# A gated linear-attention and feed-forward kernel: early weight sums of M2, their stores' queue, and the order of the residual loads

## The chip, the cores and the metric

The kernel runs on one core of one Trainium2 chip. The metric is the device time of one execution in microseconds (us). Before the change the median of three runs is 762.07 us (761.8 to 762.79).

The core has five engines that run their own instruction streams in order: TensorE (PE: matmuls into PSUM), VectorE (DVE), ScalarE (ACT), GpSimd (POOL) and SyncE (SP, which here only starts DMA transfers). ScalarE and GpSimd can start transfers too; each such start is an instruction in their streams. Engines wait for each other, and for transfers, by semaphores. Transfers started by SP and ScalarE share eight semaphores in turn: a transfer that takes one over first waits until the transfer that used it before has landed.

## What is computed

```python
x = A_x; xn = layernorm(x)                       # [1, 2048, 1024]
q, k, v = split(xn @ wqkv)                       # 32 heads of 32
s = (phi(q) @ (phi(k)^T v)) / (phi(q) @ sum phi(k)) @ wo     # linear attention
g = silu((silu(xn @ w_gate) * (xn @ w_up)) @ w_down)         # F = 3584
return x + s * g
```

## The kernel before, in words

Up to about 246 us the kernel does the layer norm and the attention; it writes s to a DRAM buffer, s_dram. After that comes the feed-forward part, in two **passes** over 1024 tokens each (p = 1, then p = 0). Every product there is done with seven block products instead of eight (a Winograd form of Strassen's method), so each weight tile needs four sums of its blocks, T1 to T4.

**Weights in packs.** Gate and up weights, and w_down, are read raw once; their sums are made during the first pass, and what results goes to DRAM as packs (pk_g, pk_u for gate and up, and wd: "a" packs with four quarters and "b" packs with three). All packs travel through one pool, wgu, of eight buffers (tile name w_sb). load_w_to(n) (L270) issues loads up to the n-th pack of a fixed list; each waits until the buffer it gets has been released by its last readers. In the first pass SP's order is the scheduler's, within the due points at which the program calls load_w_to; in the last pass's gate and up part SP's order is the one written down. The other engines follow the written order throughout.

**Each pass** first does 28 gate and up steps (i = 0 to 27, two per 256 columns of F). Then the first pass multiplies by w_down in emit_down (L1220), with token tiles in two pairs (hf = 0: tiles 0, 1; hf = 1: tiles 2, 3). Each pair runs over k = 0 to 13, the second tile LEAD = 6 steps behind the first, so a loop has NS = 20 steps st. There are four loops: "a" products for hf = 0, "a" for hf = 1, then "b" products for hf = 1, which add to the same PSUM banks, and "b" for hf = 0 ("fresh", in new banks). In the a loop of hf = 1 the b packs are loaded, each into the buffer of an a pack that the second tile has just finished (L1365). In the fresh loop the next pass's packs are loaded likewise (L1394).

evac_a (L1272) takes a tile's "a" products out of PSUM: ScalarE copies x (L1282), VectorE adds y and zw (L1283 to L1288), ScalarE applies SiLU (L1290). evac_b (L1294) adds the "b" products (L1302, L1308: tile dd). For hf = 1 the b products write again to the banks dx and dzw that evac_a reads. next_S and emit_Ssum (L705) make sums of activations on VectorE, for the later steps of the loop and for the next pass.

**The last pass** instead uses emit_down_m (L1409): seven products M1 to M7 (order 1, 2, 7, 6, 5, 4, 3), and M1, M2, M4 and M5 are split once more by the same method (l2_M). For these four, sums of w_down's packs are needed again. Those of M1 and M5 are made on GpSimd during the last pass. Those of M2 and M4 are made **early**, in the b loops of the first pass's emit_down, by l2_early (L1118): from b pack j (j = 0 to 6) it makes four sums on VectorE (L1136, 128 x 256) into an unused part of the same buffer, and later stores quarters and sums to DRAM (l2_2, l2_4) with three transfers (L1128 to L1130, 448 KB in all) on SP's queue. The sums of M4 overwrite those of M2. The loop that drives it is L1382 to L1386: M2's sums at steps 3 to 9 of the first b loop, stored three steps later; M4's at steps 10 to 16, stored two steps later.

**Residual tiles.** The end of both passes is fin (L1210): y = y * s (L1214) and x + y (L1215) on VectorE, then the store to the output (L1216), on GpSimd's queue in the first pass and on SP's in the last. x and s come in tiles of 128 x 512 (io_load, L1197: two loads of 128 KB on SP, L1205 and L1206) in a pool of five buffers (iop). There are 32 such tiles in a list fq. Five are loaded during the first pass; after that every fin loads the next one, which must wait until that fin's output has landed, since it takes the same buffer. In emit_down, two fins follow each pair of evac_a, six the hf = 1 b loop, three the fresh loop, and the last three are put off ("deferred") to steps 0, 1 and 2 of the next pass. In emit_down_m, four fins run during M7, four at the start of M3's products (fill3), and eight after that.

Of the kernel before, what the change touches and what calls it, by code (L numbers as in the profile page):

```python
# [21 lines left out]
def kernel(  # L22
# [247 lines left out]
    def load_w_to(n):  # L270
        while w_next[0] < min(n, len(w_seq)):
            load_w()
# [680 lines left out]
    with ExitStack() as p3:  # L953
# [164 lines left out]
        def l2_early(M, j, store):  # L1118

            t = w_tiles[(passes[0], "b", j)][:].rearrange("p h a b -> p (h a b)")  # L1120
            q = M_PACK[M][1]
            w = t[:, 0:6 * CW].rearrange("p (k q c n) -> p q k c n", k=2, q=3, c=2)[:, q]
            T = t[:, 6 * CW:8 * CW].rearrange("p (b n) -> p b n", b=4)
            if store:
                if M not in l2_drams:
                    l2_drams[M] = dram.tile([P, 7, NQ, CH], BF16, name="l2_%d" % M)
                d = l2_drams[M]
                nc.sync.dma_start(out=d[:, 0:2, j], in_=w[:, :, 0])  # L1128
                nc.sync.dma_start(out=d[:, 6, j], in_=w[:, 1, 1])
                nc.sync.dma_start(out=d[:, 2:6, j], in_=T)  # L1130
                return
            r = w.bitcast(F16) if M >= 4 else w
            t1, t2, t3, t4 = [T[:, i].bitcast(F16) for i in range(4)]
            for o_, a_, b_ in ((t1, r[:, 0, 1], r[:, 0, 0]), (t2, r[:, 1, 1], t1), (t3, r[:, 1, 1], r[:, 0, 1]),
                               (t4, r[:, 1, 0], t2)):
                nc.vector.tensor_tensor(out=o_, in0=a_, in1=b_, op=ALU.subtract)  # L1136
# [57 lines left out]
                for t in (2 * hf, 2 * hf + 1):  # L1194
                    fq += [(p, t + TPB, 0), (p, t, 1), (p, t, 0)]

        def io_load(after=None):  # L1197
            if not fq:
                return
            p, t, cc = key = fq.pop(0)  # L1200
            r0 = p * TB2 + t * P
            pool, tg = iop, "io"
            io = pool.tile([P, 2, CW], BF16, name="io", tag=tg)
            eng = nc.sync
            gate([eng.dma_start(out=io[:, 0, :], in_=x2[r0:r0 + P, cc * CW:(cc + 1) * CW]),  # L1205
                  eng.dma_start(out=io[:, 1, :], in_=s_dram[r0:r0 + P, cc * CW:(cc + 1) * CW])],  # L1206
                 after, sync=True)
            io_tiles[key] = io

# [10 lines left out]
        def emit_down(p, h, base, last, more_S, next_S):  # L1220
# [121 lines left out]
                    fin(p, t, 0, g11, *fin_e, cols=cs)  # L1342

            NS = NFG + LEAD
            for hf in range(2):
                t0, t1 = 2 * hf, 2 * hf + 1
                for st in range(NS):
                    if st == 4:
                        while pend:
                            pend.pop(0)()  # L1350
                    if hf == 0:
                        for m in {4: (4,), 8: (5, 6)}.get(st, ()):
                            more_S(m)
                        if st in (12, 14, 16):
                            next_S((st - 12) // 2)
                    elif st % 2 == 0 and 3 <= st // 2 + 2 < NWA:
                        next_S(st // 2 + 2)
                    if st < NFG:
                        step_a(t0, st)
                        if st == NFG - 1:  # L1360
                            evac_a(t0, hf == 0)
                    if st >= LEAD:
                        step_a(t1, st - LEAD)
                        if hf == 1 and (st - LEAD) % 2 == 1:
                            load_w_to(base + NWA + (st - LEAD) // 2 + 2)  # L1365
                evac_a(t1, hf == 0)
                if hf == 0:
                    load_w_to(base + NWA + 1)
# [4 lines left out]
            for hf in (1, 0):  # L1373
                t0, t1 = 2 * hf, 2 * hf + 1
                fresh = hf == 0
                endz = last and fresh
                for st in range(NFG if endz else NS):
                    if st == 4:
                        while pend:
                            pend.pop(0)()  # L1380
                    if not last:
                        for M, q0, dq, lag in zip(L2_EARLY, (3, 10), (1, 1), (3, 2)):  # L1382
                            for d, store in ((0, False), (lag, True)):
                                j, rem = divmod(st + (1 - hf) * NS - q0 - d, dq)
                                if rem == 0 and 0 <= j < NQ:
                                    l2_early(M, j, store)  # L1386
                    if st < NFG:
                        step_b(t0, st, fresh)
                        if st == NFG - 1:
                            fins = evac_b(t0, fresh)  # L1390
                    if st >= LEAD and not endz:
                        step_b(t1, st - LEAD, fresh)
                        if fresh and (st - LEAD) % 2 == 1:
                            load_w_to(base + 2 * NWA + (st - LEAD) // 2 + 2)  # L1394
                if endz:
                    for f in fins:
                        f()
                    finish(t1)
                    break
                fins2 = evac_b(t1, fresh)  # L1400
                for f in fins:
                    f()
                if fresh:
                    deferred.extend(fins2)
                else:
                    for f in fins2:
                        f()

        def emit_down_m(p, h, base):  # L1409
# [165 lines left out]
            for t in range(TPB):  # L1575
                if t:
                    prod_t(7, t, M7[t], True)
                tt(KB[t], M7[t], KA[t])
                flush(1)
            load(7)  # L1580
            sums(S4, A12, S2, ALU.subtract)
            l2_lhs_all(5, quads(h, 0, 1).bitcast(F16), nc.vector)
# [25 lines left out]
            def fill3():  # L1608
                for t in range(TPB):
                    fins.append((t + TPB, 1, silu(T5[t], "g22")))  # L1610
                flush()
                M3.extend(banks())
                out3(0)
# [21 lines left out]
        for pi, p in enumerate(passes):  # L1635
# [81 lines left out]
            for i in range(n):  # L1717
                if first:
                    load_w_to(base + i + (na0 if i < n - 7 else 8 if i > n - 6 else 7))
                else:  # L1720
                    load_w_to(base + i + (5 if i < 17 else 6))
                if i + 1 < n:
                    emit_a(keys[i + 1])
                    emit_c22(keys[i + 1])
# [40 lines left out]
                        l2_lhs(2, quads(h, 1, 0), i // 4 - 1, nc.gpsimd)  # L1765
                if deferred:
                    deferred.pop(0)()
            sp_man.close()
            base += n
            if last_pass:  # L1770
# [37 lines left out]
```

## Time and profile before

| what | value |
|---|---|
| median of 3 runs | 762.07 us |
| the profiled execution: its time, its span | 762.54 us, 760.8 us |
| TensorE busy | 741.0 us, 97% of the span |
| VectorE, ScalarE, GpSimd busy | 592.1, 385.2, 356.4 us |
| DMA, mean over the span | 253 GB/s |
| granted TensorE clock, mean | 0.995 |
| first pass's emit_down | 414.3 to 500.9 us |
| last pass's gate and up steps | 500.9 to 671.8 us |
| emit_down_m, last matmul, end of span | 671.8, 751.05, 760.8 us |

The profile is one execution, recorded by the hardware. "L1242" is line 1242 of the kernel. A row of the timeline gives start, duration, engine, line, operation, output and inputs, how many instructions it merges, and in brackets how long the engine was idle before it and what ended that. "SPq" rows are transfers being started; a transfer lands later. A line of the chain of waits gives start, duration and what ran. A line of the waits of an engine gives the waiting engine and line, who it waited for, total us, times and longest. A line of the table by stretches gives the stretch, its length, then busy us (and instructions) of PE, PEld, DVE, ACT and POOL, the granted clock, the busy share of the 16 DMA engines and GB/s.

### The profile page before, as it was taken

The numbers are of one execution on the slowest core, as the hardware profiler recorded it, in microseconds if no ns is written. First come the engines' busy times: TensorE is split into PE (matmuls) and PEld (weight loads), VectorE is DVE, ScalarE is ACT, GpSimd is POOL, SyncE is SP. The second block draws the span as 40 slices with busy tenths as digits, with TensorE's granted clock in tenths as the row PEclk, the third lists the DMA queues.
The fourth block names the chain that finished last, engine by engine and source line by source line (L and its number), as shares of the span: only waits on it lengthen the run. The fifth ranks groups of instructions, "written<-read, shape, count | busy, mean of one in ns | idle before, by whom it ended". The sixth has DMA issues, their size and how long they took to land.

```text
span 760.8 us, 11165 instructions
## 1 busy us (share of the span) xinstructions
PE 741.0 (97%) x3835; PEld 365.0 (48%) x3899; DVE 592.1 (78%) x1119; ACT 385.2 (51%) x557; POOL 356.4 (47%) x444
## 2 busy tenths in 40 slices
PE   8999999999999999999999999999999999999994
PEld 3544544444544444444444444444444444476582
DVE  6687787886796788888889757767687777778975
ACT  5677776988956565666659201132323222231033
POOL 2444799998540276858675000110764655330000
PEclk9999999999999999999999999999999999999997
DMA  9957799869679667888899249988898875458755
GB/s 315 300 149 135 236 327 306 293 159 276 209 173 307 225 226 270 313 286 313 268 346 400 68 142 315 282 290 314 322 337 280 290 241 173 157 184 290 246 191 159
DMA packets 134425, 192.37 MB, mean 253 GB/s; under 512 B 36480, under 2 KB 108928, under 8 KB 124640
## 3 DMA queue, kind: packets, MB, share of 16 engines
q1 hardware_dynamic: 127024, 160.59, 66.0%
q0 software_dynamic: 5904, 28.58, 9.8%
q10 hardware_dynamic: 1440, 2.49, 1.0%
q8 instruction: 30, 0.49, 0.3%
q14 instruction: 27, 0.22, 0.1%
HBM read 120.85 MB, written 63.44 MB: 242 GB/s over the span
## 4 chain that ended last, share of the span: by engine, by line
PE 88%; DVE 5%; DMA 4%; issue 1%; ACT 1%; SPq 0%; DVEq 0%; ACTq 0%
PE zw L967 25%; PE kv_ps L555 14%; PE xb L967 12%; PE q_ps L183 6%; PE yb L967 6%; PE dzw L1242 5%; PE dm L1481 4%; PE dm L1445 3%; PE fx L817 3%; PE s_ps L775 2%; PE dx L1242 2%; PE dy L1242 2%; DVE w_sb L1136 1%; PE kvz L577 1%; PE nd L744 1%
## 5 line engine op out<-in xcount | busy, mean ns | idle before, releaser
L967 PEld LDWEIGHTS <-w_sb 128*128 128x128 f16 (+1 forms) x1568 | 152.0, 98 | 184.6 <-DMA w_sb<-pk_g 2.0
L967 PE MATMUL xb<-xnT,w_sb 128*128 128x512 bf16 x420 | 113.3, 379 | 1.5
L555 PE MATMUL kv_ps<-wkv_sb,xnT 128*128 128x512 bf16 x499 | 112.9, 379 | 1.2 <-ACT xnT L544 0.4
L967 PE MATMUL zw<-S,w_sb 128*128 128x512 f16 x448 | 105.8, 379 | 0.0
L967 PE MATMUL zw<-xnT,w_sb 128*128 128x512 bf16 x448 | 105.8, 379 | 0.0
L322 POOL TENSOR_TENSOR w_sb<-w_sb 128x512 f16<-128x512 bf16 x42 | 50.7, 1208 | 95.5 <-DVE w_sb L310 51.3
L287 ACT ACTIVATE w_sb<-w_sb 128x2048 bf16<-128x2048 bf16 x42 | 79.9, 1902 | 4.1 <-DMA w_sb<-in_B_w_up_dram 3.0
L555 PEld LDWEIGHTS <-xnT 128*128 128x128 bf16 x512 | 48.3, 98 | 55.9 <-ACT xnT L544 0.8
L967 PE MATMUL yb<-S,w_sb 128*128 128x512 f16 x224 | 57.5, 379 | 1.6 <-DMA w_sb<-pk_g 1.5
L183 PE MATMUL q_ps<-xnT,wq_sb 128*128 128x512 bf16 x249 | 58.0, 379 | 0.8 <-DVE pqT L151 0.4
L1043 ACT ACTIVATE sg<-cg 128x1024 bf16<-128x1024 f32 x28 | 29.6, 1057 | 57.4 <-DVE cg L1036 57.4
L1216 POOL DMA_DIRECT2D out_dram<-io x16 | 8.7, 544 | 106.2 <-DVE io L1215 105.7
L1036 DVE SCALAR_TENSOR_TENSOR cg<-zw,rc_all,s 128x1024 f32<-128x1024 f32 x28 | 35.9, 1283 | 25.4 <-PE zw L967 13.2
L995 DVE SCALAR_TENSOR_TENSOR s<-yb,rc_all,s 128x512 f32<-128x512 f32 x42 | 31.4, 748 | 28.1 <-ACT s L994 28.1
L1148 POOL TENSOR_TENSOR w_sb<-w_sb 128x512 f16<-128x512 bf16 (+3 forms) x32 | 35.9, 1143 | 35.2 <-DMA w_sb<-wd 34.3
L323 POOL TENSOR_TENSOR w_sb<-w_sb 128x512 f16<-128x512 bf16 x42 | 50.8, 1209 | 3.3
L325 POOL TENSOR_TENSOR w_sb<-w_sb 128x512 f16<-128x512 bf16 x42 | 50.4, 1199 | 0.0
L324 POOL TENSOR_TENSOR w_sb<-w_sb 128x512 f16<-128x512 bf16 x42 | 49.9, 1188 | 0.0
L994 ACT ACTIVATE s<-xb,rcl 128x512 f32<-128x512 f32 x14 | 9.6, 687 | 65.8 <-PE xb L967 65.8
L1242 PE MATMUL dx<-w_sb,hT 128*128 128x512 bf16 x108 | 40.9, 379 | 0.2
L994 ACT ACTIVATE s<-xb,rc_all 128x512 f32<-128x512 f32 x42 | 28.4, 676 | 22.9 <-issue 12.7
L310 DVE TENSOR_SCALAR w_sb<-w_sb,cs_all 128x2048 bf16<-128x2048 bf16 x35 | 36.3, 1037 | 2.8
(228 smaller groups left out, 1324.4 us busy)
## 6 DMA issues: line engine op xcount, KB each, us to landing
w_sb<-pk_g SPq DMA_DIRECT2D x27, 1024.0 KB, 6.6
pk_g<-w_sb SPq DMA_DIRECT2D x14, 1024.0 KB, 5.2
w_sb<-pk_u SPq DMA_DIRECT2D x14, 1024.0 KB, 7.6
pk_u<-w_sb POOLq DMA_DIRECT2D x13, 1024.0 KB, 5.4
w_sb<-l SPq DMA_DIRECT2D x12, 896.0 KB, 4.6
w_sb<-in_B_w_gate_dram SPq DMA_DIRECT2D x14, 512.0 KB, 6.6
w_sb<-in_B_w_down_dram SPq DMA_DIRECT2D x28, 256.0 KB, 4.6
w_sb<-in_B_w_up_dram SPq DMA_DIRECT2D x14, 512.0 KB, 5.4
```

The lines of the kernel that those rows point to most:

```text
L183: nc.tensor.matmul(q_ps[:], lhsT=wq_sb[:, dc, g * P:(g + 1) * P], rhs=xn_ap(dc, btok), start=(dc == 0), stop=(dc == DC - 1))
L287: nc.scalar.activation(out=junk, in_=raw_view(key, t), func=ACT.Square, accum_out=asum[:])
L310: nc.vector.tensor_scalar(out=w, in0=w, scalar1=cs_all[:, c:c + 1], scalar2=None, op0=ALU.mult)
L322: nc.gpsimd.tensor_tensor(out=T1, in0=b12, in1=b11, op=ALU.subtract)
L323: nc.gpsimd.tensor_tensor(out=T2, in0=b22, in1=T1, op=ALU.subtract)
L324: nc.gpsimd.tensor_tensor(out=T3, in0=b22, in1=b12, op=ALU.subtract)
L325: nc.gpsimd.tensor_tensor(out=T4, in0=b21, in1=T2, op=ALU.subtract)
L555: mm = nc.tensor.matmul(kv_ps[:], lhsT=xn_ap(dc, tok), rhs=wkv_sb[:, dc, c * CW:(c + 1) * CW], start=(dc == 0), stop=(dc == DC - 1))
L967: mm = nc.tensor.matmul(out, lhsT=lhs(k), rhs=rhs(k), start=(first and k == 0), stop=(k == HK - 1), skip_group_check=True)
L994: nc.scalar.activation(out=s1[:], in_=x_[:], func=ACT.Copy, scale=rc)
L1036: nc.vector.scalar_tensor_tensor(out=d12, in0=zw[:], scalar=rc, in1=s2[:, None, :].to_broadcast([P, 2, TB]), op0=ALU.mult, op1=ALU.add)
L1242: nc.tensor.matmul(out, lhsT=lhs, rhs=rhs, start=first, stop=lastk, skip_group_check=True)
```

## The change

Three edits, none of them to a matmul.

1. l2_early's stores are issued by ScalarE instead of SP, and M2's sums come sooner. Counting steps n through the a loop of hf = 1 (0 to 19) and the two b loops (20 to 59), M2's sums of pack j move from n = 23 + j to n = 8 + 2j, stored two steps later; M4's from n = 30 + j to n = 25 + j, still stored two steps later.
2. Residual loads are held back. After the first of the six fins of the hf = 1 b loop, the following loads wait in a list until step 11 of the fresh loop; those of the deferred fins are issued three steps i later, after that step's load_w_to. So they stand behind pack loads in SP's queue.
3. The last seven residual tiles no longer rotate through the five io buffers. Three are loaded ahead of M5's last loads in the written order, into the dead buffer S2 and two dead buffers of the activation pool; four in fill3, into buffers of the pack pool.

```diff
@@ l2_early
-                nc.sync.dma_start(out=d[:, 0:2, j], in_=w[:, :, 0])
-                nc.sync.dma_start(out=d[:, 6, j], in_=w[:, 1, 1])
-                nc.sync.dma_start(out=d[:, 2:6, j], in_=T)
+                nc.scalar.dma_start(out=d[:, 0:2, j], in_=w[:, :, 0])
+                nc.scalar.dma_start(out=d[:, 6, j], in_=w[:, 1, 1])
+                nc.scalar.dma_start(out=d[:, 2:6, j], in_=T)
@@ io_load
-        def io_load(after=None):
-            if not fq:
+        io_due = deque()
+        hold = [False]
+
+        def io_load(after=None, pool=None, tg=None):
+            if not fq or len(fq) <= 7 and pool is None:
+                return
+            if hold[0] and after is None:
+                io_due.append(hold[0])
                 return
             p, t, cc = key = fq.pop(0)
             r0 = p * TB2 + t * P
-            pool, tg = iop, "io"
-            io = pool.tile([P, 2, CW], BF16, name="io", tag=tg)
-            eng = nc.sync
...
+            if pool is wgu:
+                io = w_slot()[:].rearrange("p h a b -> p (h a b)")[:, 0:2 * CW].rearrange("p (q n) -> p q n", q=2)
+            else:
+                io = (pool or iop).tile([P, 2, CW], BF16, name="io", tag=tg or "io")
...
@@ emit_down
             NS = NFG + LEAD
+            def early(n):
+
+                for M, at, lag in ((2, lambda j: 8 + 2 * j, 2), (4, lambda j: NS + 5 + j, 2)):
+                    for j in range(NQ):
+                        if n in (at(j), at(j) + lag):
+                            l2_early(M, j, n > at(j))
+
             for hf in range(2):
                 t0, t1 = 2 * hf, 2 * hf + 1
                 for st in range(NS):
+                    if not last and hf == 1:
+                        early(st)
...
                     if not last:
-                        for M, q0, dq, lag in zip(L2_EARLY, (3, 10), (1, 1), (3, 2)):
-                            for d, store in ((0, False), (lag, True)):
-                                j, rem = divmod(st + (1 - hf) * NS - q0 - d, dq)
-                                if rem == 0 and 0 <= j < NQ:
-                                    l2_early(M, j, store)
+                        early(NS * (2 - hf) + st)
...
+                        if fresh and st == LEAD + 5:
+                            hold[0] = False
+                            while io_due:
+                                io_due.popleft()
+                                io_load()
...
                 for f in fins:
                     f()
+                    hold[0] = -1 if not fresh and not last else False
@@ emit_down_m, ahead of load(7)
+            io_load(None, sp, "S2")
+            for _ in range(2):
+                io_load(None, xnp, "xn8")
             load(7)
@@ fill3
                     fins.append((t + TPB, 1, silu(T5[t], "g22")))
+                for _ in range(TPB):
+                    io_load(None, wgu)
                 flush()
@@ the last pass's gate and up steps
                     load_w_to(base + i + (5 if i < 17 else 6))
+                    hold[0] = False
+                    while io_due and io_due[0] <= i:
+                        io_due.popleft()
+                        io_load()
+                    hold[0] = i + 3
```

More of the change, by code (lines that the diff above doesn't have):

```diff
@@ L1201, in io_load @@
             r0 = p * TB2 + t * P
-            pool, tg = iop, "io"
-            io = pool.tile([P, 2, CW], BF16, name="io", tag=tg)
-            eng = nc.sync
-            gate([eng.dma_start(out=io[:, 0, :], in_=x2[r0:r0 + P, cc * CW:(cc + 1) * CW]),
-                  eng.dma_start(out=io[:, 1, :], in_=s_dram[r0:r0 + P, cc * CW:(cc + 1) * CW])],
+            if pool is wgu:
+                io = w_slot()[:].rearrange("p h a b -> p (h a b)")[:, 0:2 * CW].rearrange("p (q n) -> p q n", q=2)
+            else:
+                io = (pool or iop).tile([P, 2, CW], BF16, name="io", tag=tg or "io")
+            gate([nc.sync.dma_start(out=io[:, 0, :], in_=x2[r0:r0 + P, cc * CW:(cc + 1) * CW]),
+                  nc.sync.dma_start(out=io[:, 1, :], in_=s_dram[r0:r0 + P, cc * CW:(cc + 1) * CW])],
                  after, sync=True)
@@ L1767 @@
                     deferred.pop(0)()
+            hold[0] = False
+            while io_due:
+                io_due.popleft()
+                io_load()
             sp_man.close()
```

## The prediction

> **What bounds the kernel now.** I read the page first: its engine totals, then the waits of TensorE, then the stretches in which TensorE is idle, then the rows around them.
>
> ```profile
> span 760.8 us, 11165 instructions
> PE 741.0 (97%) x3835; PEld 365.0 (48%) x3899; DVE 592.1 (78%) x1119; ACT 385.2 (51%) x557; POOL 356.4 (47%) x444
> ```
>
> TensorE is busy 741.0 of 760.8 us. No matmul is changed, so only its 20 idle us can be won. The waits of TensorE name two inside the region of the change, and the table by stretches shows the rest:
>
> ```profile
> PE dzw L1242 <- DVE dd L1308: 1.8, 1, 1.8
> PE yb L967 <- DMA w_sb<-pk_g: 1.5, 1, 1.5
> ```
>
> ```profile
> 459.00:485.00 26.00, 24.11 (x111) 10.94 (x112) 21.43 (x67) 4.44 (x6) 1.08 (x2) 1.00 0.98 311
> 751.00:761.00 10.00, 0.05 (x1) 0.00 (x0) 4.67 (x13) 1.45 (x3) 0.00 (x0) 0.61 0.54 166
> ```
>
> The first line of the table says that while VectorE is late (459 to 485 us), the DMA engines are 98% busy. The second says that after 751 us TensorE does nothing: the last ten us are eviction, residual and stores. Of TensorE's other idle time, 4.7 us lie before 250 us, which the change does not touch. So three places can move: the 1.8 at 481 us, the 1.5 at 510.5 us, the 9.7 at the end.
>
> **The end: the last seven residual tiles.** The timelines of TensorE, VectorE and SP after 741 us:
>
> ```profile
> 741.79 9.26 PE L1445 MATMUL dm<-w_sb,hT 128*128 128x512 bf16 x55
> ```
>
> ```profile
> 745.08 0.69 DVE L1433 TENSOR_TENSOR c<-dm,kA 128x512 f32<-128x512 f32 x1 [1.70 <-PE dm L1445]
> 748.28 0.43 DVE L1214 TENSOR_TENSOR g<-g,io 128x512 bf16<-128x512 bf16 x1 [2.51 <-DMA io<-s_dram]
> ...
> 752.27 0.68 DVE L1433 TENSOR_TENSOR c<-dm,kA 128x512 f32<-128x512 f32 x1
> ...
> 757.62 0.23 DVE L1215 TENSOR_TENSOR io<-g,io 128x128 bf16<-128x128 bf16 x1
> ```
>
> TensorE ends at 751.05. VectorE had its operands at 745.8 but sat 2.51 us for a residual tile, because the five io buffers come free only when earlier outputs have landed; then it waited 0.97, 0.19 and 0.79 us more. The change loads these seven tiles into buffers that are dead by then. In the program's order the last four pairs stand behind M3's weights, whose issues end at 730.5 (SP row 724.08, 6.39 us); the latest buffer is freed by a product of M4 that ends near 734.3. With 2.5 us to landing (median of the io loads after 690 us) all seven are there by 739, and the first is used at 745.8. Then: 745.08 + 0.69 = 745.77; five residual pairs last 3.99 us as before (748.28 to 752.27), to 749.76; the next c 0.69, to 750.45 (its matmuls end at 748.0); its SiLU 0.72, to 751.17; one pair 0.80, to 751.97; the last pair in two parts 1.15 (756.70 to 757.85), to 753.1. Before, VectorE ended at 757.85. What follows, 2.95 us to the span's end, stays. **Gain 4.7 us.** What is late next is VectorE itself, 2 us behind TensorE. The cost of the loads is nothing as long as DMA has room, which is 0.44 busy from 729 to 751; without room the first waits come back, up to the 4.7.
>
> **The packs at 510 us.** In SP's order before, the pack loads for the next pass stand behind the early stores and residual loads:
>
> ```profile
> 504.48 0.33 SPq L1205 DMA_DIRECT2D io<-in_A_x_dram  x1
> 504.87 0.44 SPq L1206 DMA_DIRECT2D io<-s_dram  x1
> 505.40 0.39 SPq L264 DMA_DIRECT2D w_sb<-pk_g  x1
> ```
>
> This pk_g lands 6.6 us later and TensorE gets it at 512.08, 1.54 late. Its slot was free after the second tile's fourth step of the last half, near 492. In the changed program's order the first two packs stand ahead of the sixth residual pair, and the other held pairs behind a third pack. Issued at 494 and landing within 9.0 us (the longest pack of this stretch that did not queue behind other packs) it is there by 503: **gain 1.5 us**. The held pairs then come later. What they may delay is VectorE's sixth residual pair, which blocked VectorE to 496.74 before too, with TensorE unharmed: the next eviction is needed at 502.6. ScalarE's last SiLUs of that half now queue behind 42 DMA issues (below) and may slip from 483 to some 487; their banks are needed at 500.9, so this costs nothing.
>
> **The early sums.** Moved: 24 of M2's 28 sums (a row of 40 takes 9.41, so 0.235 us each) go from behind the next pass's S sums to between next_S and the two evictions evac_a; M4's 28 stay, some steps earlier. Moved to ScalarE's queue: 42 stores. ScalarE's own issues cost 0.33 to 0.37 us in this trace (s_dram, L781), 15 us in all, and it is idle 13.9 us before 456 and 10.3 after 466. The gain: VectorE from the second evac_a to dd has 12 sums less, 2.8 us, more than the 1.8 of the wait. But the moved sums bring a **new wait**: M2's sum for pack j waits for b pack j, and VectorE works in order. The loads keep their times, since each waits for an a slot: the sixth is issued at
>
> ```profile
> 459.38 6.67 DMA w_sb<-wd
> ```
>
> ```profile
> 462.81 0.69 DVE L1283 TENSOR_TENSOR s<-dy,s 128x512 f32<-128x512 f32 x1 [3.83 <-PE dzw L1242]
> ...
> 481.66 1.22 DVE L1308 TENSOR_TENSOR dd<-dzw,s 128x1024 f32<-128x1024 f32 x1
> ```
>
> and landed at 466.05, whereas the second evac_a started at 462.81. In the changed order that evac_a stands behind the sixth pack's sums. On ScalarE its copy stands behind the stores of packs 3 to 5, and one of them waits for the semaphore that this very load uses. Behind both stands TensorE: it writes the second tile's dzw again at 467.38.
> Working: landing. These 768 KB loads take 5.7 us in the median (4.8 to 8.2 among the four of this stretch). I take 5.7, so 465.1: the load before it lands sooner, since its SP queue no longer carries stores; but ScalarE's stores now run beside it. Two more issues on ScalarE, 0.8, copy at 465.9; copy to third sum 2.83 (456.15 to 458.98 in the first evac_a): evac_a ends at 468.8 instead of 465.0. TensorE stops for 1.4 us at 467.4. From there to the matmul behind dd: before, 465.02 to 481.66 is 16.64; less 12 sums, 2.82; plus dd to TensorE, 1.28 (482.94 less 481.66): 15.1. So that matmul comes at 483.9 against 482.94: **loss 1.0 us**, and the wait on dd is not gone but has a second one ahead of it. Bounds: with 4.8 to landing the loss is 0.1; with 8.2 it is 3.5; if ScalarE is held by a store that takes 8.9 (the longest of L1128) from 460.4, evac_a ends at 472.5 and the loss is 4.7. If nothing holds evac_a, the gain is the whole 1.8.
> The other moved waits are covered: the first sums delay next_S by 0.9 of 4.5 us that it is early; the first evac_a waits for pack 2 (landed 455.7) and has three us to spare.
>
> The trace shows what one queue does: three stores issued on SP at 463.2 to 464.6 landed after 8 to 9 us, together with the pack issued ahead of them. [...] I know of no row here with stores on ScalarE's queue beside such loads.
>
> **Sum.** The profiled execution took 762.54 (span 760.8 and 1.74 around it), 0.47 above the median of 762.07. -4.7 - 1.5 + 1.0 = -5.2: 757.3 for that execution, **756.9** against the median.
>
> **Rivals.**
> No new wait: the sixth b pack lands by 463.6, evac_a is in time, and the dd wait goes: -4.7 - 1.5 - 1.8 = -8.0, 754.1. For it: DMA is only 0.43 busy from 414 to 459. Against it: none of the four loads took under 4.8.
> Most of it given back: stores or loads at their longest, 3.5 to 4.7 lost: 759.3 to 760.6. For it: 98% busy DMA.
> Slower: the same place, evac_a, with the b pack starved by ScalarE's stores as packs are when queued deep: 14.4 us to landing (the pk_g issued at 508.18). It lands at 473.8, evac_a ends at 477.5, the loss is 477.5 + 15.1 - 482.94 = 9.7: 765.6. It decides once the landing takes more than about 11 us. Against it: only two or three such loads are ever in flight.
> The change does not do what it says: SP stands still on a slot or a semaphore, and the seven tiles come no sooner. Then only +1.0 - 1.5: 761.6.
>
> **How the numbers follow.** About 0.2% (1.5 us) is what a measurement of this kernel can tell from no change. Forecast (loss 0.1 to 3: 756 to 759) 0.48; no new wait 0.2; most given back 0.14; slower 0.09; the tail unchanged 0.09. Range 753.8 to 760.6: it reaches over the first three and leaves out the last two. Faster by over 0.2% (below 760.5): the first three, 0.82; within: 0.10, with a little of the neighbours; slower 0.08.
>
> **What would show it.** Right: after 741 us no VectorE wait on io, and VectorE ends some 2 us after TensorE; no TensorE wait on pk_g; pk_g issued before 496; a TensorE wait on evac_a (L1289 or L1295) of some 1.4 us near 467 and one on dd near 482. Wrong: a b pack that lands before 464 or after 468, a TensorE wait in the first steps of the next pass, or residual pairs that still wait after 745.

## The result, and the profile after

| | before | after |
|---|---|---|
| median of 15 runs | 762.39 us (761.19 to 763.5) | 760.59 us (759.3 to 762.98) |
| the profiled execution: its time, its span | 762.54, 760.8 | 762.85, 761.1 |
| last matmul, VectorE's last instruction | 751.05, 757.85 | 756.06, 758.15 |

The ratio is 0.998 with a 95% interval of 0.997 to 0.9989: a gain of 0.8 to 2.3 us, where 5.2 were forecast. The profiled execution of the changed kernel is one of the longest of its 15, 2.3 above their median. So its trace shows where time was lost, and shows more of it than the median run lost.

First the page and the waits of TensorE:

```profile
span 761.1 us, 11166 instructions
PE 744.4 (98%) x3835; PEld 365.9 (48%) x3899; DVE 592.2 (78%) x1119; ACT 384.3 (50%) x557; POOL 352.2 (46%) x444
```

```profile
PE dx L1249 <- ACT s L1289: 2.8, 1, 2.8
PE dzw L1249 <- DVE s L1295: 1.9, 1, 1.9
...
PE zw L967 <- DVE s L1009: 0.8, 1, 0.8
```

The same number of recorded matmuls, 3835, kept TensorE busy 3.4 us longer than before: it ran some of them slower. The waits on dd (1.8) and on pk_g (1.5) are both gone. In their place stand 4.7 us at the second evac_a (L1289 is ScalarE's copy of dx, L1295 the third sum) and 0.8 on L1009, one of the first evictions of the next pass.

The end came out as forecast. VectorE after 750 us, then TensorE's last row:

```profile
750.70 0.42 DVE L1221 TENSOR_TENSOR g<-g,w_sb 128x512 bf16<-128x512 bf16 x1
751.15 0.42 DVE L1222 TENSOR_TENSOR w_sb<-g,w_sb 128x512 bf16<-128x512 bf16 x1
...
757.93 0.22 DVE L1222 TENSOR_TENSOR w_sb<-g,w_sb 128x128 bf16<-128x128 bf16 x1
```

```profile
746.80 9.26 PE L1463 MATMUL dm<-w_sb,hT 128*128 128x512 bf16 x55
```

No residual pair waits on io, so there is no bracket behind them. VectorE ends at 758.15, 2.1 us after the last matmul (756.06), and the span 5.0 us after it instead of 9.75: 4.7 us won. They were spent before that: the last matmul came 5.0 us later than before the change.

Where they were spent is seen in three timelines around 467 us: ScalarE ("ACTq" rows are stores that it issues), VectorE, TensorE.

```profile
461.65 0.59 ACTq L1128 DMA_DIRECT2D l<-w_sb  x1
466.30 0.34 ACTq L1129 DMA_DIRECT2D l<-w_sb  x1
...
468.78 0.41 ACTq L1130 DMA_DIRECT2D l<-w_sb  x1
469.23 0.58 ACT L1289 COPY s<-dx 128x512 f32<-128x512 f32 x1 [8.36 <-DMA l<-w_sb]
```

```profile
466.41 1.02 DVE L1136 TENSOR_TENSOR w_sb<-w_sb 128x256 f16<-128x256 bf16 x4 [1.38 <-DMA w_sb<-wd]
469.85 0.69 DVE L1290 TENSOR_TENSOR s<-dy,s 128x512 f32<-128x512 f32 x1 [2.42 <-ACT s L1289]
...
471.37 0.69 DVE L1295 TENSOR_TENSOR s<-dzw,s 128x512 f32<-128x512 f32 x1
```

```profile
469.87 0.38 PE L1249 MATMUL dx<-w_sb,hT 128*128 128x512 bf16 x1 [2.82 <-ACT s L1289]
472.12 1.01 PE L1249 MATMUL dzw<-w_sb,hT 128*128 128x512 f16 x2 [1.87 <-DVE s L1295]
472.92 0.63 PE L1249 MATMUL dx<-w_sb,hT 128*128 128x512 bf16 x1
```

ScalarE issued the first store of pack 3 at 461.65 and the second only at 466.30. In the written order that second store takes over the semaphore of a store of pack 1 (the trace's records name the same one for both), issued at 455.37, which took 10.9 us to land: 466.27. Four more issues followed, and then the copy. VectorE had begun the sums of the sixth pack at 466.41 and was idle 2.42 us for the copy; it ended evac_a at 472.06. Before the change, with no stores on ScalarE, the same copy ran as soon as dx was done:

```profile
462.19 0.59 ACT L1282 COPY s<-dx 128x512 f32<-128x512 f32 x1 [2.40 <-PE dx L1242]
```

The last two rows of TensorE show something that no wait names: two matmuls that took 0.59 us before the stop take 1.01 after it, one of 0.38 takes 0.63. The table by stretches has the granted clock (third number from the end):

```profile
472.00:474.00 2.00, 1.88 (x5) 0.69 (x5) 1.97 (x4) 0.72 (x1) 0.00 (x0) 0.50 1.03 329
474.00:476.00 2.00, 2.00 (x6) 0.68 (x5) 1.97 (x3) 0.00 (x0) 0.00 (x0) 0.50 0.93 276
476.00:478.00 2.00, 2.00 (x7) 0.74 (x6) 1.97 (x6) 0.00 (x0) 0.00 (x0) 0.57 0.21 62
478.00:480.00 2.00, 2.00 (x11) 0.88 (x9) 1.90 (x7) 0.00 (x0) 0.79 (x2) 1.00 0.60 168
```

For nearly six us after the stop TensorE was granted half its clock: 5, 6 and 7 matmuls in two us instead of 11. From the first dzw matmul behind evac_a to the last one of emit_down: 472.12 to 505.95, 33.83 us. Before the change: 467.38 to 500.42, 33.04 us, of which 1.79 waiting on dd, so 31.25. The low clock cost the difference, 2.6 us.

The wait on L1009 is followed back in the chain of waits (start, duration, what):

```profile
494.76 5.07 DMA out_dram<-io
...
500.28 5.94 DMA io<-s_dram
...
515.34 1.89 PE zw L967 x8
```

and on VectorE:

```profile
497.23 0.42 DVE L1222 TENSOR_TENSOR io<-g,io 128x512 bf16<-128x512 bf16 x1
506.25 0.42 DVE L1221 TENSOR_TENSOR g<-g,io 128x512 bf16<-128x512 bf16 x1 [8.60 <-DMA io<-s_dram]
...
507.05 1.22 DVE L1309 TENSOR_TENSOR dd<-dzw,kept 128x1024 f32<-128x1024 f32 x1
```

The first output of the six leaves at 494.8, because ScalarE's SiLUs of the two b evictions ran only from 491.83, when the last of the 42 stores was issued. The sixth residual pair takes that output's buffer, lands at 506.2, and VectorE, in order, does the fresh loop's first eviction behind it, at 507.05. Before the change it was at 497.54:

```profile
497.54 1.22 DVE L1302 TENSOR_TENSOR dd<-dzw,kept 128x1024 f32<-128x1024 f32 x1
```

The sum for this execution: -4.7 (end) - 1.5 (pk_g) - 1.8 (dd) + 4.7 (evac_a) + 2.6 (clock) + 0.8 (L1009) = +0.1; measured +0.3.

### The profile page after: what moved, and what is told of

Its sections match the earlier page's. It is cut to its first block, busy times and chain, and to the rows that moved or that the text cites. A ratio compares the mean times of both kernels' runs of the same rounds, so it can differ in the third digit from the quotient of the medians.

```text
span 761.1 us, 11166 instructions
## 1 busy us (share of the span) xinstructions
PE 744.4 (98%) x3835; PEld 365.9 (48%) x3899; DVE 592.2 (78%) x1119; ACT 384.3 (50%) x557; POOL 352.2 (46%) x444
## 4 chain that ended last, share of the span: by engine, by line
PE 85%; issue 8%; DVE 4%; DMA 1%; ACT 1%; POOL 0%; SPq 0%; DVEq 0%; ACTq 0%; POOLq 0%
PE zw L967 25%; PE kv_ps L555 14%; PE xb L967 12%; PE q_ps L183 6%; PE yb L967 6%; PE dm L1499 6%; PE dm L1463 4%; PE fx L817 3%; PE s_ps L775 2%; PE dzw L1249 1%; PE kvz L577 1%; PE nd L744 1%; DMA io<-s_dram 1%; DVE g L1221 1%; PE dy L1249 1%
## 5 line engine op out<-in xcount | busy, mean ns | idle before, releaser
L995 DVE SCALAR_TENSOR_TENSOR s<-yb,rc_all,s 128x512 f32<-128x512 f32 x42 | 31.5, 749 | 29.1 <-ACT s L994 29.1
L1036 DVE SCALAR_TENSOR_TENSOR cg<-zw,rc_all,s 128x1024 f32<-128x1024 f32 x28 | 35.9, 1284 | 23.1 <-PE zw L967 12.4
L1148 POOL TENSOR_TENSOR w_sb<-w_sb 128x512 f16<-128x512 bf16 (+3 forms) x32 | 33.1, 1055 | 36.3 <-DMA w_sb<-wd 31.8
```

## The experiments

The theory at this point: ScalarE's stores, and not the b pack, hold the second evac_a; the tail's gain is whole. The rivals: VectorE behind the b pack, as I had put it; the traffic of the stores; the hold of the residual loads. All ratios below are to the kernel before on the same chip. L1009, L995 and L1036 are VectorE's evictions in the next pass's gate and up steps (L995 stands ahead of L1009). Kernels without the hold have lines from 1206 on three lower.

| kernel | median us | ratio (95%) | TensorE's waits from 400 us on in its profiled execution |
|---|---|---|---|
| changed kernel | 760.59 | 0.998 (0.997 to 0.9989) | 2.8 + 1.9 evac_a, 0.8 L1009 |
| tail alone | 758.38 | 0.9947 (0.9934 to 0.996) | 1.8 dd, 1.2 pk_u |
| tail and hold | 759.45 | 0.9958 (0.9942 to 0.9975) | 1.8 dd, 1.4 L1009 |
| stores on SP | 758.85 | 0.9958 (0.9944 to 0.9973) | 2.3 evac_a, 1.3 dd |
| stores on GpSimd | 764.94 | 1.0031 (1.0015 to 1.0048) | 3.9 evac_a, 3.5 L1009 |
| M2's stores behind evac_a | 766.51 | 1.0055 (1.0043 to 1.0067) | 1.2 evac_a, 5.1 dd, 2.2 L1309 |
| no hold | 760.88 | 0.9987 (0.9975 to 0.9999) | 1.1 + 1.9 evac_a, 1.3 dd, 0.8 L1009 |
| four early packs | 756.84 | 0.9931 (0.9919 to 0.9943) | 2.4 L1009 |
| four early packs, no hold | 756.12 | 0.9921 (0.9909 to 0.9933) | 0.3 dd, 1.4 L995 by the view (a pack, see below) |
| the same, stores on ScalarE | 756.92 | 0.9933 (0.9914 to 0.9953) | 1.5 dd, 0.7 L1009 and L1036 |
| the same, late stores of M4 | 756.51 | 0.9926 (0.9905 to 0.9947) | 1.2 dd, 2.6 pk_u |
| the same, six pairs put off | 756.36 | 0.9925 (0.9908 to 0.9942) | 1.3 dd |

**Tail alone.** The kernel before with the third edit.

```diff
+            if not fq or len(fq) <= 7 and pool is None:
+                return
...
+            io_load(None, sp, "S2")
+            for _ in range(2):
+                io_load(None, xnp, "xn8")
             load(7)
...
+                for _ in range(TPB):
+                    io_load(None, wgu)
                 flush()
```

> The kernel before with the third edit alone (the last seven residual tiles in dead buffers). Theory (the tail gain is whole, and what was lost lies at the second evac_a): 762.4 less 4.7, so about 757.7; the time from the last matmul to the end of the span is some 5.0 us instead of 9.75, and TensorE's waits are those of before (1.8 on dd, 1.5 on pk_g). Rival (the seven loads disturb the transfers of M3 and M4, and part of the gain is given back earlier): 759 to 761, with a TensorE wait on a pack after 690 us.

Measured 758.38, 3.9 below the kernel before. In its profile the last matmul is at 751.34 and the span ends at 756.6, 5.3 after it: 4.5 won there. Ahead of it 0.3 was lost (the last matmul came that much later than before); TensorE's waits from 400 us on are those of before (1.8 on dd, and 1.2 on a pack, here pk_u). The theory holds: the tail alone gives more than the whole change.

**Tail and hold.** The changed kernel, sums and stores of M2 and M4 as before.

```diff
-                        early(NS * (2 - hf) + st)
+                        for M, q0, dq, lag in zip(L2_EARLY, (3, 10), (1, 1), (3, 2)):
...
-                nc.scalar.dma_start(out=d[:, 0:2, j], in_=w[:, :, 0])
+                nc.sync.dma_start(out=d[:, 0:2, j], in_=w[:, :, 0])
```

> The changed kernel with its first edit undone: sums and stores of M2 and M4 as before, on SP; residual loads held, last seven tiles in dead buffers. Theory (the second evac_a, with stores on ScalarE ahead of its copy, is what cost the difference): no stall at 467 us, 1.8 on dd as before, no wait on pk_g, so 762.4 - 4.7 - 1.5 = 756.2. Rival (the hold itself makes the residual pairs late and through them the first evictions of the next pass): a TensorE wait of some 0.8 near 514 us, and 757 to 758.5.

```profile
PE dzw L1249 <- DVE dd L1315: 1.8, 1, 1.8
PE zw L967 <- DVE s L1009: 1.4, 1, 1.4
```

Measured 759.45. My theory missed by 3 us. The rival has the mechanism, and even its range ends 1 us lower: the hold takes the wait on the pack away and puts one on L1009 in its place. VectorE:

```profile
501.89 0.68 DVE L1310 TENSOR_TENSOR c<-dx,kept 128x512 f32<-128x512 f32 x1
505.05 0.43 DVE L1221 TENSOR_TENSOR g<-g,io 128x512 bf16<-128x512 bf16 x1 [2.48 <-DMA io<-s_dram]
...
509.08 0.75 DVE L1009 SCALAR_TENSOR_TENSOR s<-zw,rc_all,s 128x512 f32<-128x512 f32 x1
```

The fresh loop's residual pairs, held behind packs, come 2.48 us late, and L1009 stands behind them. Before, the same pairs began at 502.79 with no wait, and L1009 ran at 506.80. Against the tail alone the hold shows no gain (the intervals overlap).

**Stores on SP.**

```diff
-                nc.scalar.dma_start(out=d[:, 0:2, j], in_=w[:, :, 0])
-                nc.scalar.dma_start(out=d[:, 6, j], in_=w[:, 1, 1])
-                nc.scalar.dma_start(out=d[:, 2:6, j], in_=T)
+                nc.sync.dma_start(out=d[:, 0:2, j], in_=w[:, :, 0])
+                nc.sync.dma_start(out=d[:, 6, j], in_=w[:, 1, 1])
+                nc.sync.dma_start(out=d[:, 2:6, j], in_=T)
```

> The changed kernel with the stores of M2 and M4 back on SP's queue, the sums as early as in the changed kernel. Theory (ScalarE was held by stores that wait for a semaphore of an earlier store): ScalarE copies dx as soon as it is done, near 463 us; the second evac_a then waits only for the sums of the sixth b pack on VectorE, so the stop of TensorE falls from 4.7 to 2.6 us or less and the granted clock stays near 1.0 after it; 755.5 to 758, unless SP, which now carries the stores again, loads the packs later. Rival (VectorE stands behind the b pack, whatever queue the stores are on): the stop stays at 4 us or more, and the time at 760.6.

```profile
466.30 1.02 DVE L1136 TENSOR_TENSOR w_sb<-w_sb 128x256 f16<-128x256 bf16 x4 [1.51 <-DMA w_sb<-wd]
467.24 0.68 DVE L1290 TENSOR_TENSOR s<-dy,s 128x512 f32<-128x512 f32 x1
...
468.75 0.69 DVE L1295 TENSOR_TENSOR s<-dzw,s 128x512 f32<-128x512 f32 x1
```

The stop is 2.3 us instead of 4.7, it is all VectorE's, and the clock stays at 1.00 behind it (460 to 500 us). What went, 2.4, is what VectorE had sat idle for the copy (2.42). The sixth pack's sums begin at 466.30, against 466.41 with the stores on ScalarE: between these two queues the issuing engine made no difference to the pack. Here the mechanism of my prediction is seen alone: evac_a ends at 469.4, forecast 468.8; the matmul behind dd starts at 484.56, 15.1 later as worked out. But 2.3 + 1.3 of stops is 1.8 more than the 1.8 of before; with no wait left near 510 us (1.5 before), that nearly cancels. The time, 758.85, is that of the tail alone, 0.85 above the theory's range: ScalarE's queue explains half of the stop, and the late packs the other half.

**Stores on GpSimd.** The same three lines with nc.gpsimd.

> The changed kernel with the stores of M2 and M4 issued by GpSimd, which has almost nothing to do between 414 and 500 us. Theory (ScalarE's queue): the stop at 467 us falls to 2.6 us or less, the SiLUs of the two b evictions run when their operands are ready (near 484 and 488 us instead of 492 to 495), the sixth residual pair no longer comes late: 755 to 757. Rival (the b pack, or the traffic of the stores): the stop stays at 4 us or more; 760.6.

Measured 764.94, slower than before, and neither side foresaw it. An issue takes GpSimd 0.6 to 0.8 us, and outputs of the b eviction stand behind the stores:

```profile
492.52 0.75 POOL L1130 DMA_DIRECT2D l<-w_sb  x1
493.27 2.70 POOL L1223 DMA_DIRECT2D out_dram<-io  x5
```

The residual sums of five of the six had been done by 491.4. So the outputs, the sixth residual pair and the next pass's first evictions are late just as in the changed kernel: 3.5 us on L1009. Both stops (3.9 at 471 us, 3.5 at 515.5) are followed by a granted clock near 0.5 for some 3 us (0.50 and 0.71 in the stretches of 2 us from 472 to 476, 0.53 and 0.61 from 516 to 520, 1.00 behind each). The stop at evac_a is VectorE's alone, and it comes from the pack:

```profile
467.73 1.02 DVE L1136 TENSOR_TENSOR w_sb<-w_sb 128x256 f16<-128x256 bf16 x4 [1.82 <-DMA w_sb<-wd]
```

The sixth pack took 8.8 us to land here, against 7.2 in the changed kernel and in the one with the stores on SP, and its sums began 1.3 us later. So of the two sides the rival (the b pack, or the traffic of the stores) has the cause of this stop; what made the pack slower with this queue is not shown.

**M2's stores behind the second evac_a**, still on ScalarE.

```diff
-                for M, at, lag in ((2, lambda j: 8 + 2 * j, 2), (4, lambda j: NS + 5 + j, 2)):
+                for M, at, put in ((2, lambda j: 8 + 2 * j, lambda j: NS + j), (4, lambda j: NS + 5 + j, lambda j: NS + 7 + j)):
```

> The changed kernel with M2's stores still on ScalarE's queue, but put behind the second evac_a in the written order (pack j at n = 20 + j). Theory (the copy of evac_a stood behind stores that waited for an earlier store's landing): no TensorE wait on L1289; what is left of the stop is the wait for the sixth pack's sums, some 2.3 us as with the stores on SP, and the granted clock stays at 1.0 behind it. The 42 stores now stand together ahead of the SiLUs of the b evictions, so the sixth residual pair stays late and with it the wait near 514 us: 758 to 760. Rival (the traffic of the stores makes the stop, not the place in the queue): with less traffic before 467 us the stop falls below 1.5 us. Other rival (the stop has nothing to do with ScalarE): it stays at 4 us or more.

```profile
462.04 0.58 ACT L1289 COPY s<-dx 128x512 f32<-128x512 f32 x1 [2.40 <-PE dx L1249]
```

```profile
PE dzw L1249 <- DVE dd L1315: 5.1, 1, 5.1
PE zw L967 <- DVE dd L1309: 2.2, 1, 2.2
PE dzw L1249 <- DVE s L1295: 1.2, 1, 1.2
```

The copy runs as soon as dx is done, 7.2 us sooner than in the changed kernel, and no wait on it is left. The stop falls to 1.2, near the 1.4 that I had forecast for VectorE alone (evac_a ends at 468.5). That is less than the 2.3 of the stores on SP; here the sixth pack's sums begin at 465.37, some 0.9 sooner, so a part of the difference may be the traffic, as the first rival has it, whose number (below 1.5) came true. That the place in the queue held the copy is shown. The total, 766.5, was foreseen by none: the sums of M4 overwrite those of M2, so VectorE now waited for M2's late stores, and dd with it:

```profile
482.07 1.02 DVE L1136 TENSOR_TENSOR w_sb<-w_sb 128x256 f16<-128x256 f16 x4 [1.50 <-DMA l<-w_sb]
485.20 1.02 DVE L1136 TENSOR_TENSOR w_sb<-w_sb 128x256 f16<-128x256 f16 x4 [2.11 <-DMA l<-w_sb]
```

**No hold.** The changed kernel without

```diff
-            if hold[0] and after is None:
-                io_due.append(hold[0])
-                return
```

> The changed kernel with the second edit undone (residual loads not held back). Theory: the stop at 467 us stays (4.7 us, and the clock behind it); the wait of 0.8 us on L1009 near 514 us goes or shrinks, since the sixth pair and the three deferred ones are loaded sooner; and as SP carries no stores, the packs are in time all the same: 759.5 to 760.5, about half a us less than the changed kernel. Rival (the hold is what keeps the packs in time): a TensorE wait on pk_g or pk_u of 1 us or more near 510 us, and a time at or above the changed kernel's 760.6.

Measured 760.88, that of the changed kernel. No wait on a pack came, so with SP free of the stores the hold was not needed for the packs; and the 0.8 on L1009 stayed, because the sixth pair's buffer is given by an output that is late through ScalarE's SiLUs (the first on dd at 490.33 in this trace, against 482.98 before), not by SP's order. I had expected that wait to go, which it did not, and the stop at 467 us to stay at 4.7 with the low clock behind it: in this trace it is 3.0, the clock stays at 1.00, and 1.3 on dd comes after it.

**Four early packs.** Stores on SP, only packs that land before the second evac_a are summed ahead of it.

```diff
-                for M, at, lag in ((2, lambda j: 8 + 2 * j, 2), (4, lambda j: NS + 5 + j, 2)):
+                for M, at, put in ((2, lambda j: 8 + 2 * j if j < 4 else NS + j, lambda j: 10 + 2 * j if j < 4 else NS + 2 + j), (4, lambda j: NS + 8 + j, lambda j: NS + 10 + j)):
```

> The changed kernel with the stores on SP, and of M2's sums only those of packs 0 to 3 moved ahead of the second evac_a (n = 8 + 2j; packs 4 to 6 at n = 20 + j), M4's sums at n = 28 + j, each stored two steps later. Theory (the loss at evac_a came from packs 4 and 5, which land at 464 and 466.3 us): no stop at 467 us; between the second evac_a and dd VectorE has 8 sums less than before (1.9 us), so dd's wait of 1.8 us is gone too; the wait on L1009 near 510 us (1.4 us with the sums of before) is left: 762.4 - 4.5 - 1.8 = 756. Rival (the sums are not what makes dd late): dd's wait stays near 1.8 us, 758 to 759.5.

Measured 756.84. There is no stop at 467 us, none on dd, and 2.4 on L1009 is the only wait left from 400 us on. The theory holds.

**Four early packs, no hold.**

> The same as the kernel with four early packs, without the hold of the residual loads. Theory (the hold exchanges a wait on a pack for a wait on the next pass's first eviction): near 510 us TensorE waits 1 to 2 us for a pack instead of for L1009, and the time is within 0.5 us of the kernel with the hold, near 756. Rival (the hold is worth what I forecast, 1.5 us): 757.5, with no such wait in the kernel that holds.

Measured 756.12, the lowest median of all: 6.2 below the kernel before and 4.5 below the changed one. The time is the theory's, and so is the mechanism, though the view of waits hides it: it puts 1.4 us near 504 us down to L995. The rows of SP, of the weight loads ("PEld") and of the matmuls are

```profile
496.38 0.40 SPq L264 DMA_DIRECT2D w_sb<-pk_u  x1
...
503.53 1.41 PEld L967 LDWEIGHTS <-w_sb 128*128 128x128 f16 x8 [1.94 <-DMA w_sb<-pk_u]
503.53 1.04 PE L967 MATMUL yb<-S,w_sb 128*128 128x512 f16 x4 [1.45 <-DVE s L995]
```

The weights of that matmul are this pk_u. It landed at 503.49, 7.1 us after its issue, and the weight load ahead of the matmul waited for it; L995 only happens to end at the same time, at 503.53. A wait of a matmul is to be read together with that of its weight load. With the hold, the same pack was issued at 491.72 and landed at 497.79, in time, and there the wait of 2.4 on L1009 stands. So the hold brings the pack 5.7 us sooner and exchanges a wait on it for one on VectorE; it bought nothing here either, and whether it cost something is within the intervals.

**The same, stores on ScalarE.** The three lines with nc.scalar again, nothing else.

> The kernel with four early packs and no hold (756.1 us), with one thing changed: the stores are issued by ScalarE instead of SP. Theory (ScalarE's queue is what costs: an engine that must copy and apply SiLU in order stands behind stores that wait for earlier stores to land): the SiLUs of the b evictions run some 6 us later than the 482 to 485 us they have with SP, the sixth residual pair and with it the first evictions of the next pass come late, and where a store of packs 0 to 3 is held, the copy of the second evac_a is late too: 758.5 to 761.5. Rival (the queue is of no account, only the moved sums of packs 4 and 5 were): within 0.8 us of 756.1.

```profile
461.52 1.50 ACTq L1129 DMA_DIRECT2D l<-w_sb  x1
463.06 0.71 ACTq L1130 DMA_DIRECT2D l<-w_sb  x1
463.81 0.59 ACT L1286 COPY s<-dx 128x512 f32<-128x512 f32 x1 [3.62 <-issue]
```

Measured 756.92, at the rival's bound of 0.8 and far from the theory's 758.5. The copy is 1.5 us late and the SiLUs end at 492.4, as the theory has it, but evac_a had that much to spare, and TensorE stops for only 1.5 on dd. So ScalarE's queue is not always dear by itself. In the changed kernel the sums of packs 4 and 5 and the stores of pack 4 stood ahead of the one evac_a that TensorE needed next; here they do not. How long a store is held also differs from run to run. The second store of pack 3 went out at 461.52 here and at 466.30 in the changed kernel, because the store of pack 1 whose semaphore it takes over took 6.0 us to land here and 10.9 there. In the kernel without the hold that store took 5.8, and it was the first store of pack 4 that held the copy: it went out at 465.87, behind a store of pack 2 that took 6.9 from 458.99.

**The same as four early packs without hold, M4's last stores later.**

```diff
-(4, lambda j: NS + 8 + j, lambda j: NS + 10 + j)
+(4, lambda j: NS + 8 + j, lambda j: NS + 10 + j if j < 3 else NS + 19 + j)
```

> The kernel with four early packs and no hold (756.1 us), with M4's stores of packs 3 to 6 put nine steps later, behind the residual loads of the six fins in SP's order. Theory (what is left near 504 us, 1.4 us on L995, comes from the sixth residual pair, which SP issues only behind the last stores, at 490.6 us): the pair is loaded some 3 us sooner, VectorE is free by 491.5, the wait goes, 754.7. Rival (the stores then stand beside the next pass's packs): a TensorE wait of 1 to 2 us on pk_g or pk_u near 505 us, and 756 to 757.

Measured 756.51, no different. The sixth pair came 1.7 us sooner (492.88 instead of 494.56), but the wait near 504 us was the pack's and not the pair's, so the theory's wait was the wrong one. In the profiled execution, which is the longest of the six (759.88), 2.6 on pk_u stand there. In SP's order that pack now stands behind the last stores that were put off: it was issued at 500.19, right behind a store at 499.63, and landed at 506.09; in the kernel without this edit it was issued at 496.38 and landed at 503.49. That is the rival's mechanism, seen in one execution.

**The same, all six pairs of the fresh loop put off.**

```diff
                 fins2 = evac_b(t1, fresh)
+                if fresh:
+                    deferred.extend(fins + fins2)
+                    continue
                 for f in fins:
                     f()
```

> The kernel with four early packs and no hold (756.1 us), with all six residual pairs of the fresh loop put off to steps 0 to 5 of the next pass, one a step; there the first three ran at once, between the last dd and the next pass's first L995. Theory (the 1.4 us wait on L995 near 504 us is VectorE's own order: three pairs of 0.8 us stand ahead of L995, 500.4 to 502.8 us): L995 starts some 2.4 us sooner, the wait goes, and the time is 754.7. Rival (the pairs, put off, delay the evictions of the next steps as much, or the packs of these steps are late anyway): a wait of 1 us or more between 504 and 525 us on another line, and 756 or more.

No wait came near 504 us, nor any after it up to the end, but not because L995 came sooner:

```profile
503.46 1.04 PE L967 MATMUL yb<-S,w_sb 128*128 128x512 f16 x4
...
503.77 0.75 DVE L995 SCALAR_TENSOR_TENSOR s<-yb,rc_all,s 128x512 f32<-128x512 f32 x1 [1.86 <-ACT s L994]
```

The matmul ran ahead of L995, so it does not need it. What it needs, the first pk_u, landed at 503.41, as late as before (503.49); TensorE itself came later, by 1.3 us that it had waited on dd, and its weight load waited only 0.45 for the pack. The edit took away a wait of VectorE on which TensorE did not stand, and the median, 756.36, is that of the kernel without it, as the rival has it: the packs of these steps are late anyway. The 1.3 us on dd come from pack 3, whose sums began at 462.35 here and at 461.36 there; evac_a and dd stand behind them. What stays open is this variation: among the kernels with four early packs dd's wait is 0 to 1.5 us, as that pack lands (or, with the stores on ScalarE, as the copy is held), and it covers gains of this size.

## Why the prediction was wrong, point by point

In the terms of the sum, for the profiled execution: the end -4.7, as forecast; the packs -0.7 instead of -1.5; the early sums +5.5 (4.7 + 2.6 - 1.8) instead of +1.0. The third is where the forecast failed.

**The end: right.** Forecast 4.7; 4.7 in the trace of the changed kernel, 4.5 in that of the tail alone, 3.9 in the medians of the latter. VectorE is what is late next, 2.1 us behind TensorE, as said.

**The packs at 510 us: the wait went, half of the gain was given back.** The step that failed: "the next eviction is needed at 502.6", with TensorE unharmed, and the SiLUs that "may slip from 483 to some 487", at no cost. I set the stores' issues on ScalarE end to end, 0.33 to 0.37 each. Measured, they are mostly 0.4 to 0.7 apart and wait for the semaphores of older transfers (from 462.24 to 466.30 in one case), and the last SiLU ended at 495.2. From it hang the outputs, from the outputs the buffers, from these the sixth pair: VectorE was blocked to 506.25, past the 502.6 that I had named as the limit. With the stores on SP the hold alone did the same on a smaller scale (2.48 us, 1.4 on L1009). The pk_g that I wanted issued before 496 went out at 497.51, and was in time all the same. I followed the moved loads to VectorE's next eviction, but not to the one after it.

**The early sums: the mechanism right, the price wrong.** The place was right (evac_a's second tile at 467 us), and without ScalarE's stores ahead of the copy so was the size: 1.2 us where they are put behind it, 2.3 with the stores on SP, against 1.4 forecast. The step that failed: "Two more issues on ScalarE, 0.8, copy at 465.9". The copy ran at 469.23. I had let ScalarE be released by the landing of the sixth pack's load, at 465.1, with two issues left. By the semaphores in the trace it was released by a store of pack 1, at 466.3, with five issues left, which took 2.9. I had written the case down as a bound (a store of 8.9 us, evac_a at 472.5; measured 10.9 and 472.06), and took the middle. The stores of packs 1 to 3 run beside b-pack loads with the 16 DMA engines fully busy (363 GB/s from 460 to 467 us), and most stores of packs 3 and 4 take over the semaphore of a store two packs older; that chain, and not only the pack, should have been priced.

**Not in the sum: the granted clock.** I put it at nothing, without a reason. The stop of 4.7 cost TensorE 4.7 and, in this execution, 2.6 more. About half of the 2.6 would have been lost otherwise: at full clock TensorE would have come to the matmul behind dd at 485.9 (an estimate: 472.12 plus the 13.8 that this took before, without the wait), and dd ended at 487.1, so some 1.3 of waiting, as with the stores on SP.

**dd.** Forecast: not gone, a second wait of 1.0 net. The 15.1 us from evac_a to dd hold in both traces (472.06 to 487.13, where dd ends; with the stores on SP 469.44 to 484.56, where the matmul behind it starts). In the changed kernel no wait is seen there only because TensorE itself was late by its clock.

**Rivals.** "Most of it given back" named this outcome, 759.3 to 760.6 with evac_a ending at 472.5 by a store of ScalarE. It got 0.14 and was the case. That the median also lies within its range, and within the stated range by 0.01 us, is in part luck: neither priced the clock or L1009. "Slower" had the right place and did not come, since the b pack was never starved (6.0 to 7.2 us to landing). The chance of "most of it given back" was too low: the changed kernel puts nine stores ahead of that copy, between 460 and 469 us, when the DMA engines were fully busy (350 GB/s over these nine us).

## What to carry to other kernels

Before a transfer is moved to the queue of an engine that computes, list what that engine must do next in order, and when the transfer's semaphore was last used: the issues around 467 us took ScalarE 0.34 to 0.68 us each, but waiting for an older transfer cost 4.1 here in the profiled execution. Early work is worth as much as its operands are early: four packs summed ahead of the eviction cut the 1.8 us wait on dd to between 0 and 1.5, and two more that landed 1.5 to 4 us after the eviction was due brought stops of 3.6 us instead (with the stores on SP). Price a new stop of the busiest engine with the clock that it may lose behind it (2.6 us here behind a stop of 4.7), and follow a delayed load through every in-order engine up to where TensorE waits, one eviction further than the first.

## What the runs showed of the hardware

The granted clock of TensorE fell to 0.50 after some stops in the middle of the kernel and came back some 3 to 7 us later, an estimate from the clock of stretches of 2 us: 0.73, 0.50, 0.50, 0.57 and then 1.00 in the changed kernel (470 to 480 us), 0.83, 0.50, 0.82 and then 1.00 in the rows below. It fell after stops of 2.18 and 5.08 us (M2's stores behind evac_a), 2.63 (late stores of M4), 3.45 and 3.93 (stores on GpSimd) and 4.7 (the changed kernel, in two parts); it did not after 1.8 (the kernel before), 2.32 (stores on SP), 2.37 (four early packs) and 3.0 (no hold, in two parts, with one matmul between). The shortest stop that cost clock:

```profile
508.00:510.00 2.00, 0.89 (x5) 0.29 (x3) 0.98 (x3) 0.00 (x0) 0.00 (x0) 1.00 1.01 337
510.00:512.00 2.00, 0.94 (x3) 0.35 (x3) 2.00 (x3) 0.95 (x1) 0.54 (x1) 0.83 0.95 221
512.00:514.00 2.00, 2.00 (x6) 0.76 (x5) 1.97 (x4) 1.97 (x4) 0.00 (x0) 0.50 0.97 397
514.00:516.00 2.00, 2.00 (x9) 0.79 (x8) 1.93 (x6) 1.17 (x2) 1.08 (x2) 0.82 0.44 168
516.00:518.00 2.00, 2.00 (x11) 0.93 (x10) 1.86 (x4) 0.69 (x1) 0.54 (x1) 1.00 0.65 235
```

This is from the kernel with M2's stores behind evac_a, around 511 us: after 2.18 us idle, six matmuls in two us, and 11 again from 516 on. The longer stop that did not, 2.37 us in the kernel with four early packs, is followed by a clock of 1.00 (508 to 520 us). So length alone does not decide; what else does is not shown here.

Between the queues of SP and ScalarE the sixth pack's times agree: its sums began at 466.41 with the stores on ScalarE and at 466.30 with them on SP. With them on GpSimd they began at 467.73; what made the pack later there is not shown.
